# One more transfer cut in two near the end of a decode attention kernel

## The chip, the cores and the metric

The kernel runs on one core of one Trainium2 chip. The metric is device time in microseconds (us), measured over several executions; lower is better.

Times "at" some us are counted from the start of the profiled span. A ratio is the mean time of one kernel's fast runs over that of the other's of the same rounds, so it is not quite the ratio of the medians quoted.

## The reference

One query per head attends to 8192 keys, for 16 heads of width 256, in bf16:

```python
B, H, Sq, Sk, D = 1, 16, 1, 8192, 256
def reference(q, k, v):
    scores = jnp.einsum("bhqd,bhkd->bhqk", q, k) * D ** -0.5
    p = softmax(scores, axis=-1)
    return jnp.einsum("bhqk,bhkd->bhqd", p, v)
```

K and V are 67 MB each and each element is used once. The kernel is a stream from memory with work hung on it.

## The kernel before

Each head's K and V is split into two halves of 2 MB (128 partitions x 32 columns x 256 elements). The halves are numbered: V28 and V29 belong to head 14, V30 and V31 to head 15. One queue, issued from SP (the sync engine), loads them in a fixed order; the last loads are V28, V29, V30, V31. A half normally comes in one transfer, but some come in several, each with its own semaphore (a counter that an engine waits on), so that work can start on the first part:

```python
FIRST_CUT = (4, 4, 8, 16)
LAST_CUT = (16, 8, 4, 4)       # V31, in columns
BEFORE_CUT = (16, 16)          # V30
...
def cuts(kind, n):
    if kind == "k" and n == 0:
        return FIRST_CUT
    if kind == "v" and n == NIT - 1:      # NIT = 32
        return LAST_CUT
    if kind == "v" and n == NIT - 2:
        return BEFORE_CUT
    return (HALF,)                        # 32 columns, 2 MB
```

The scores are made mostly on the vector engine (DVE), partly on TensorE (PE). The scalar engine (ACT) makes the exponentials and copies the outputs. The product with V is made on PE, one matmul for each column of a half. A matmul waits for the transfer that holds its column:

```python
def pv(n, c0=0, c1=HALF):
    ...
    for c in range(c0, c1):
        ...
        pe(lambda e, ...: e.matmul(a[0:1, 0:D], lhsT=E[:, col:col+1],
               rhs=Vb[slot][:, c*D:(c+1)*D], start=..., stop=...), ...,
           [f"e{h}", first_free] + landed("v", n, c, c + 1))
```

After the last keys the order of work on PE is fixed:

```python
n = 2 * (H - 2)
pv(n)                          # V28
softmax(H - 1)                 # transpose m of head 15
pv(n + 1, 0, HALF // 2)        # V29, first 16 columns
softmax2(H - 1)                # broadcast the maximum of head 15
pv(n + 1, HALF // 2, HALF)     # V29, last 16 columns
lmm(H - 1)                     # sum of head 15
n += 2
final(H - 2)                   # ACT: output of head 14
...
pv(n)                          # V30
pv(n + 1)                      # V31
final(H - 1)                   # ACT: output of head 15
```

## Time and profile before

| | before |
|---|---|
| median of 6 runs | 325.15 us (324.94 to 325.31) |
| busiest compute engine | DVE, 86% of the span |
| DMA engines | full in nearly every slice, 416 GB/s over the span |

From the page of the kernel before, its second part: the span in 40 equal slices, busy tenths for each engine, granted clock, busy share of the 16 DMA engines, and what they moved.

```profile
PE   1554328766586858686987756886665966668897
DVE  3799999999999999999998988889988889888600
PEclk9999999999698998989595989777989697897799
DMA  7999999999999999999999999999999999999993
GB/s 276 421 436 428 421 430 428 424 426 426 431 428 426 428 428 428 432 426 424 432 426 434 426 424 430 428 428 429 426 430 426 430 427 428 428 426 428 426 417 120
```

The DMA row is full from the second slice to the last but one at about 428 GB/s. The stream is the limit; the Trainium skill ("HBM Reference", Specifications (TRN2)) gives about 425 GB/s for a core that streams alone, and this trace agrees. DVE is busy too, but is done two slices before the end. So only the end of the stream and what follows it can be shortened by a change at the tail.

The trace records when each of a transfer's 16 engines signals its semaphore. The last of the 16 is the landing. Between 60 and 305 us, whole halves landed 4.90 us apart. The end of the stream:

| landing, us | V28 | V29 | V30, parts | V31, parts |
|---|---|---|---|---|
| before | 304.77 | 309.70 | 312.18, 314.66 | 317.16, 318.37, 319.01, 319.65 |

The timeline of PE in the kernel before, last 18 us. The columns are start, length, engine, line, operation, output<-inputs, shapes and count; in brackets stands the idle time before it and what ended that.

```profile
305.73 3.00 PE L607 MATMUL acc<-Vb,E 128*1 128x256 bf16 x26
308.56 0.38 PE L547 MATMUL misc<-ident,m 128*1 128x128 f32 x2
309.74 1.91 PE L607 MATMUL acc<-Vb,E 128*1 128x256 bf16 x16 [0.80 <-DMA Vb<-in_v_dram]
311.58 0.38 PE L558 MATMUL misc<-g,ones_row 1*128 1x1 f32 x2
311.89 1.91 PE L607 MATMUL acc<-Vb,E 128*1 128x256 bf16 x16
313.63 0.19 PE L587 MATMUL misc<-ones_col,lsum 128*1 128x1 f32 x2
313.69 7.17 PE L607 MATMUL acc<-Vb,E 128*1 128x256 bf16 x64
```

PE idles 0.80 us until V29 lands, and this view shows no idle time after that: the last 64 matmuls take 7.17 us, 0.112 us each. The chain of work that ended last (start, length, what) says the same: V29's landing, then PE, then the last copy on ACT.

```profile
285.68 24.02 DMA Vb<-in_v_dram
309.70 0.04 issue
309.74 1.91 PE acc L607 x16
311.65 0.31 PE misc L558 x2
311.96 1.84 PE acc L607 x16
313.80 0.03 PE misc L587 x2
313.83 7.04 PE acc L607 x64
320.87 0.02 issue
320.89 0.47 ACT o L621
```

The weight loads (PEld), at the step from V30 to V31:

```profile
313.66 3.38 PEld L607 LDWEIGHTS acc<-Vb,E 128*1 128x1 bf16 x32
317.20 3.36 PEld L607 LDWEIGHTS acc<-Vb,E 128*1 128x1 bf16 x32 [0.16 <-DMA Vb<-in_v_dram]
```

They run about 0.1 us ahead of the matmuls (the last one for V30 starts at 316.96, its matmul at 317.07), and had to wait 0.16 us for V31's first part, which landed at 317.16. At 0.112 us each, the matmuls were due there at about 317.27 and would not have waited. That is a second deadline, and the prediction put it 0.1 us behind the first.

### The profile page before, as it was taken

The page shows a single profiled execution, that of the slowest core. Times are in us where ns is not written, and L with a number is a line of the kernel's source. Part 1 is how long each engine was busy: PE and PEld are TensorE (multiplying, and loading weights), DVE is VectorE, ACT ScalarE, POOL GpSimd, SP SyncE. Part 2 cuts the span into 40 slices and gives each one's busy share as a digit, 9 for nine tenths or more (in the row PEclk, how much of TensorE's full clock was granted, in tenths as well). Part 3 has the DMA queues.
Part 4 walks back from the last instruction along what each step waited for, and adds up shares of the span by engine and source line. Part 5 has one row for each costly group of instructions (what it writes and reads, how often), then busy time and mean ns, then how long its engine had stood idle before and what let it go on. Part 6 is the DMA issues. An engine that isn't in the chain of part 4 may idle for free.

```text
span 322.9 us, 6455 instructions
## 1 busy us (share of the span) xinstructions
PE 222.2 (69%) x2166; PEld 155.6 (48%) x2166; DVE 277.8 (86%) x1607; ACT 94.1 (29%) x185; POOL 0.2 (0%) x4
## 2 busy tenths in 40 slices
PE   1554328766586858686987756886665966668897
PEld 0333225655364635454564534564543644455565
DVE  3799999999999999999998988889988889888600
ACT  3362321432324242323142242212422123232010
POOL 0000000000000000000000000000000000000000
PEclk9999999999698998989595989777989697897799
DMA  7999999999999999999999999999999999999993
GB/s 276 421 436 428 421 430 428 424 426 426 431 428 426 428 428 428 432 426 424 432 426 434 426 424 430 428 428 429 426 430 426 430 427 428 428 426 428 426 417 120
DMA packets 10271, 134.37 MB, mean 416 GB/s; under 512 B 1154, under 2 KB 1171, under 8 KB 1940
## 3 DMA queue, kind: packets, MB, share of 16 engines
q1 hardware_dynamic: 10224, 134.22, 98.1%
q8 instruction: 5, 0.08, 0.1%
q14 instruction: 6, 0.05, 0.0%
q10 hardware_dynamic: 36, 0.02, 0.0%
HBM read 134.23 MB, written 0.01 MB: 416 GB/s over the span
## 4 chain that ended last, share of the span: by engine, by line
DVE 52%; DMA 37%; PE 5%; issue 5%; DVEq 1%; ACT 0%; SPq 0%
DVE prod L360 48%; DMA Kb<-in_k_dram 19%; DMA Vb<-in_v_dram 18%; PE acc L607 5%; DVE S L360 2%; DVE g L332 1%; DVE colf L286 0%; DVE recip L341 0%; DVEq L145 0%; DVE m L379 0%; ACT o L621 0%; DVEq L138 0%; DVEq L139 0%; SPq L319 0%; PE misc L558 0%
## 5 line engine op out<-in xcount | busy, mean ns | idle before, releaser
L360 DVE CUSTOM_DVE_ANT_0 prod<-Kb,qbc 128x256 bf16<-128x256 bf16 x768 | 269.1, 411 | 24.6 <-DMA Kb<-in_k_dram 15.7
L607 PE MATMUL acc<-Vb,E 128*1 128x256 bf16 x1024 | 147.4, 314 | 8.8 <-DMA Vb<-in_v_dram 8.8
L607 PEld LDWEIGHTS acc<-Vb,E 128*1 128x1 bf16 x1024 | 96.3, 96 | 52.4 <-DMA Vb<-in_v_dram 9.9
L502 ACT ACTIVATE KT<-tp 128x1024 bf16<-128x1024 bf16 x64 | 62.0, 1021 | 118.2 <-PE tp L493 118.2
L360 DVE DVE_READ_ACCUMULATOR2_ANT S<- 128x1 f32 x768 | 56.8, 74 | 0.0
L493 PE MATMUL tp<-identb,Kb 128*128 128x128 bf16 x512 | 38.2, 234 | 7.8 <-DMA Kb<-in_k_dram 7.8
L493 PEld LDWEIGHTS tp<-identb,Kb 128*128 128x128 bf16 x512 | 32.3, 105 | 15.7 <-issue 14.2
L519 PE MATMUL spe<-qcur,KT 128*128 128x1 bf16 x512 | 20.6, 165 | 19.7 <-ACT KT L502 19.7
L558 PE MATMUL misc<-g,ones_row 1*128 1x1 f32 x32 | 7.1, 287 | 36.1 <-DVE g L332 36.1
L519 PEld LDWEIGHTS spe<-qcur,KT 128*128 128x128 bf16 x512 | 16.4, 99 | 24.5 <-ACT KT L502 24.3
L621 ACT ACTIVATE o<-acc,recip 1x256 bf16<-1x256 f32 x16 | 7.4, 464 | 69.4 <-PE acc L607 69.4
L558 PEld LDWEIGHTS misc<-g,ones_row 1*128 1x128 f32 x32 | 5.7, 221 | 39.1 <-DVE g L332 38.8
L547 PE MATMUL misc<-ident,m 128*1 128x128 f32 x34 | 7.1, 293 | 18.6 <-DVE m L379 18.6
L547 PEld LDWEIGHTS misc<-ident,m 128*1 128x1 f32 x34 | 1.9, 82 | 22.0 <-DVE m L379 21.4
L565 ACT ACTIVATE negb<-misc 128x1 f32<-128x1 f32 x16 | 2.7, 171 | 27.4 <-PE misc L558 27.4
L332 DVE TENSOR_REDUCE g<-misc 1x1 f32<-1x128 f32 x17 | 4.7, 274 | 5.2 <-PE misc L547 5.2
L341 DVE RECIPROCAL recip<-misc 1x1 f32<-1x1 f32 x17 | 2.6, 151 | 4.6 <-PE misc L587 4.6
L572 ACT ACTIVATE E<-S,negb 128x64 bf16<-128x64 f32 x16 | 5.6, 348 | 0.7 <-ACT negb L565 0.2
L587 PE MATMUL misc<-ones_col,lsum 128*1 128x1 f32 x34 | 3.2, 164 | 3.7 <-ACT E L572 3.7
L439 ACT ACTIVATE qbc<-qb 128x256 bf16<-128x256 bf16 x14 | 5.6, 400 | 0.0
L532 ACT ACTIVATE S<-spe 128x16 f32<-128x16 f32 x16 | 2.9, 183 | 7.2 <-PE spe L519 7.2
L413 PE MATMUL tp<-q,identb 16*128 16x256 bf16 x15 | 4.1, 406 | 0.6 <-ACT qb L422 0.5
(29 smaller groups left out, 22.7 us busy)
## 6 DMA issues: line engine op xcount, KB each, us to landing
Kb<-in_k_dram SPq DMA_DIRECT2D x31, 2048.0 KB, 24.3
Vb<-in_v_dram SPq DMA_DIRECT2D x30, 2048.0 KB, 29.5
Vb<-in_v_dram SPq DMA_DIRECT2D x3, 1024.0 KB, 16.5
Kb<-in_k_dram SPq DMA_DIRECT2D x1, 1024.0 KB, 8.5
Kb<-in_k_dram SPq DMA_DIRECT2D x2, 256.0 KB, 3.0
Kb<-in_k_dram SPq DMA_DIRECT2D x1, 512.0 KB, 6.5
Vb<-in_v_dram SPq DMA_DIRECT2D x1, 512.0 KB, 12.7
Vb<-in_v_dram SPq DMA_DIRECT2D x2, 256.0 KB, 13.0
```

Of the source, the lines that this page charges most:

```text
L332: lambda e: e.tensor_reduce(g[0:1, s : s + 1], misc[s][0:1, MT0 : MT0 + P], AX.X, ALU.max),
L360: lambda e, slot=slot, c=c, col=col, h=h, r=(ttr - 1) % PROD: e.tensor_tensor_reduce(out=prod[:, r * D : (r + 1) * D], in0=Kb[slot][:, c * ...
L413: lambda e, i=i, src=src: e.matmul(bank[:, i * D : (i + 1) * D], lhsT=src[0], rhs=src[1], start=True, stop=True),
L439: lambda e: e.activation(out=qbc[:, s * D : (s + 1) * D], in_=qb[:, (h - 2) * D : (h - 1) * D], func=ACT.Copy),
L493: lambda e, c=c, hf=hf, i=(b * NH + hf) * P, view=view: e.transpose(view[:, i : i + P], Kb[slot][:, c * D + hf * P : c * D + (hf + 1) * P] ...
L502: lambda e, gn=gn, view=view: e.activation(out=KT[gn % KT_SLOTS][:, :], in_=view[:, 0 : GROUP * D], func=ACT.Copy),
L519: lambda e, b=b, hf=hf, oc=oc, gn=gn: e.matmul(spe[sl(h)][:, oc : oc + 1], lhsT=KT[gn % KT_SLOTS][:, (b * NH + hf) * P : (b * NH + hf + 1) ...
L547: lambda e: e.matmul(misc[s][0:1, MT0 : MT0 + P], lhsT=m[:, s : s + 1], rhs=ident[:, :], start=True, stop=True),
L558: lambda e: e.matmul(misc[s][:, BC0 : BC0 + 1], lhsT=ones_row[0:1, :], rhs=g[0:1, s : s + 1], start=True, stop=True),
L572: lambda e: e.activation(out=E[:, s * J : (s + 1) * J], in_=S[:, s * J : (s + 1) * J], func=ACT.Exp, bias=negb[:, h : h + 1], scale=SCALE, ...
L607: lambda e, c=c, col=col: e.matmul(a[0:1, 0:D], lhsT=E[:, col : col + 1], rhs=Vb[slot][:, c * D : (c + 1) * D], start=(x == 0 and c == 0), ...
L621: lambda e: e.activation(out=o[0:1, h * D : (h + 1) * D], in_=acc[s][0:1, 0:D], func=ACT.Copy, scale=recip[0:1, s : s + 1],),
```

## The change

The intent is to let PE start on V29 half a transfer earlier, and so remove its 0.80 us of idle time. V29 comes in two transfers of 1 MB, as V30 already does; a semaphore is added for its first part.

```diff
-        s_last = [sem(f"s_l{i}") for i in range(len(LAST_CUT) + len(BEFORE_CUT) - 2)]
+        s_last = [sem(f"s_l{i}") for i in range(len(LAST_CUT) + 2 * (len(BEFORE_CUT) - 1) - 1)]
...
-            if kind == "v" and n == NIT - 2:
+            if kind == "v" and n in (NIT - 3, NIT - 2):
                 return BEFORE_CUT
...
-                    s = sem_l[slot] if i == len(cs) - 1 else s_last[i + (len(LAST_CUT) - 1) * (n == NIT - 2)]
+                    s = sem_l[slot] if i == len(cs) - 1 else s_last[i + (len(LAST_CUT) - 2 + NIT - 1 - n if n < NIT - 1 else 0)]
```

The instructions of PE, DVE and ACT and their order are the same in both kernels. SP issues one transfer more, and one PE wait is split in two. (The diff is shortened.)

## The prediction

> **What bounds the kernel.** The page's first part has DVE busy 86%, PE 69%, but its slice table shows the 16 DMA engines full in nearly every slice at 425 to 430 GB/s: 134.22 MB of K and V come through one queue, and that stream is the limit. The landing records of the trace give one 2 MB half every 4.90 us, to the end. The change touches only the last 15 us.
>
> **The tail now** (timeline and landing records, us from the span's start). V28 (first half of head 14) lands at 304.77; V29, the half that is cut, at 309.70; V30 in two 1 MB parts at 312.18 and 314.66; V31 in parts of 1, 0.5, 0.25, 0.25 MB at 317.16, 318.37, 319.01, 319.65. PE finishes V28 and the small transpose of m at about 308.94 and then idles 0.80 us for V29 (timeline, releaser DMA Vb). From 309.74 it never stops: 16 matmuls, the broadcast of g, 16, the sum, then 64 matmuls of head 15, ending at 320.87; the last ACT copy is 320.89 to 321.36. At the full clock granted from 304.2 on, a matmul costs 0.112 us (64 in 7.17), so PE gets through V30 at about 313.69 + 3.58 = 317.27. V31's first part lands at 317.16. The weight loads even show a 0.16 us wait for DMA there. So PE has a second deadline only about 0.1 us behind the first.
>
> **What the change does.** It adds one issue on SP (0.33 us, at about 286.0, when over 20 us of transfers are queued: off the path), one semaphore, and one wait on PE. The order of work on PE, ACT, DVE is unchanged. V29's first half should land 2.47 us before its second, at about 307.2, which is before PE asks for it. The 0.80 us wait vanishes: PE starts V29 at 308.95 and its second half (due 309.70) is there by 310.8.
>
> **Where that goes.** All later PE work moves 0.8 us earlier until it meets V31: V30's second part (314.7) is needed at about 314.7, and PE is done with it at about 316.5. Then it must wait about 0.7 us for V31's first part, which cannot come earlier, since the DMA stream sets it. From 317.2 on 32 matmuls x 0.112 = 3.6 us follow, ending at 320.8. Gain at most 0.1 us. Against it: cutting costs the stream a little. V30's pair took 4.96 us, uncut halves 4.90 to 4.93, so V31 should land about 0.04 us later. The Trainium skill, "DMA: Bandwidth & Descriptors", Rules for kernel authors, asks for at least 1 MiB per DMA for bandwidth; the parts are just that, and this trace agrees that the loss is about 1%. Net: -0.05 us, within the noise of 324.94 to 325.31.
>
> **Time:** 325.15 us, 8 in 10 between 324.6 and 325.7. Faster by over 2%: 0.005; within 2%: 0.99; slower: 0.005.
>
> **What would show it.** Right: the idle of PE before V29 at 309 is gone or under 0.1 us; a new wait of PE for DMA Vb of 0.5 to 0.8 us shows at about 316.5, before the last 32 matmuls; the chain of waits ends in DMA Vb landing at about 317.2, PE x32, ACT, with x64 gone; V31's landings are where they were, within 0.15 us. Wrong: V29's first part lands after 308.9; the last 64 matmuls still run without a gap and end 0.5 us or more earlier (then V31 came earlier); or V31 lands 0.3 us or more later.
>
> **What would make it wrong.** A lower granted clock in the last 18 us (half clock was granted in 3.4 us spells until 304.2, and a spell there costs up to 1.7 us), or the extra transfer costing the queue more than the 0.05 us seen on V30.

## The result

| | before | after |
|---|---|---|
| median of 6 runs each | 325.15 us (324.94 to 325.31) | 325.20 us (324.65 to 325.47) |
| ratio of the means | 1 | 1.0001 (95%: 0.9988 to 1.0014) |
| V28's landing | 304.77 | 304.55 |
| V29's landing, its parts | 309.70 | 307.04, 309.53 |
| V30's landing, its parts | 312.18, 314.66 | 312.01, 314.50 |
| V31's first part, V31's last part | 317.16, 319.65 | 317.00, 319.50 |
| V28's landing to V31's first part | 12.39 us | 12.45 us |
| V28's landing to the start of the last ACT copy | 16.12 us | 16.19 us |

The time is the same. The last row is the measure of the tail used below. V28 is the last half that no kernel but one cuts, and counting from it takes out most of the scatter of the stream's earlier part.

The timeline of PE after, in the same stretch:

```profile
305.72 2.78 PE L607 MATMUL acc<-Vb,E 128*1 128x256 bf16 x24
308.34 0.38 PE L547 MATMUL misc<-ident,m 128*1 128x128 f32 x2
308.55 1.91 PE L607 MATMUL acc<-Vb,E 128*1 128x256 bf16 x16
310.39 0.38 PE L558 MATMUL misc<-g,ones_row 1*128 1x1 f32 x2
310.70 1.91 PE L607 MATMUL acc<-Vb,E 128*1 128x256 bf16 x16
312.44 0.19 PE L587 MATMUL misc<-ones_col,lsum 128*1 128x1 f32 x2
312.50 3.95 PE L607 MATMUL acc<-Vb,E 128*1 128x256 bf16 x32
317.05 3.65 PE L607 MATMUL acc<-Vb,E 128*1 128x256 bf16 x32 [0.59 <-DMA Vb<-in_v_dram]
```

The 0.80 us wait before V29 is gone. Counted from V28's landing, V29 starts 4.00 us after it (308.55 - 304.55) and not 4.97 (309.74 - 304.77), so 0.97 us was freed. It is lost again in two places. V30's 32 matmuls take 3.95 us where 32 unhindered ones take 3.65. And a new wait of 0.59 us stands before V31. The weight loads show both waits, at V30's second part and at V31:

```profile
314.54 1.61 PEld L607 LDWEIGHTS acc<-Vb,E 128*1 128x1 bf16 x16 [0.43 <-DMA Vb<-in_v_dram]
317.04 3.36 PEld L607 LDWEIGHTS acc<-Vb,E 128*1 128x1 bf16 x32 [0.89 <-DMA Vb<-in_v_dram]
```

The chain that ended last now runs through the landing of V31's first part, and V29 is no longer in it:

```profile
305.04 11.96 DMA Vb<-in_v_dram
317.00 0.04 issue
317.05 3.67 PE acc L607 x32
320.71 0.02 issue
320.74 0.47 ACT o L621
```

From this landing to the end of the last matmul are 3.71 us (320.71 - 317.00). In the kernel before they are the same 3.71 us (320.87 - 317.16): there too, V31's first part set the end, though the chain named V29.

### The profile page after: what moved, and what is told of

It is laid out like the page before. It is cut to its first block, busy times and chain, and to the rows that moved or that the text cites. A ratio compares the mean times of both kernels' runs of the same rounds, so it can differ in the third digit from the quotient of the medians.

```text
span 322.8 us, 6456 instructions
## 1 busy us (share of the span) xinstructions
PE 220.3 (68%) x2166; PEld 155.1 (48%) x2166; DVE 277.7 (86%) x1607; ACT 94.1 (29%) x185; POOL 0.2 (0%) x4
## 4 chain that ended last, share of the span: by engine, by line
DVE 49%; DMA 42%; issue 5%; PE 3%; DVEq 0%; ACT 0%; SPq 0%
DVE prod L360 46%; DMA Kb<-in_k_dram 27%; DMA Vb<-in_v_dram 15%; PE acc L607 3%; DVE S L360 2%; DVE g L332 0%; DVE colf L286 0%; DVE recip L341 0%; DVE m L379 0%; DVEq L145 0%; ACT o L621 0%; DVEq L138 0%; SPq L319 0%; DVEq L139 0%; DVEq L142 0%
## 5 line engine op out<-in xcount | busy, mean ns | idle before, releaser
L360 DVE CUSTOM_DVE_ANT_0 prod<-Kb,qbc 128x256 bf16<-128x256 bf16 x768 | 269.1, 411 | 24.5 <-DMA Kb<-in_k_dram 15.1
L607 PE MATMUL acc<-Vb,E 128*1 128x256 bf16 x1024 | 144.7, 310 | 8.7 <-DMA Vb<-in_v_dram 8.5
L607 PEld LDWEIGHTS acc<-Vb,E 128*1 128x1 bf16 x1024 | 95.0, 95 | 50.7 <-DMA Vb<-in_v_dram 9.9
L493 PE MATMUL tp<-identb,Kb 128*128 128x128 bf16 x512 | 38.9, 237 | 7.1 <-DMA Kb<-in_k_dram 7.1
L493 PEld LDWEIGHTS tp<-identb,Kb 128*128 128x128 bf16 x512 | 33.0, 106 | 15.2 <-issue 12.8
L422 ACT ACTIVATE qb<-tp 128x512 bf16<-128x512 f32 x7 | 3.9, 595 | 3.8 <-PE tp L413 3.8
```

Source lines behind the costliest of these rows:

```text
L360: lambda e, slot=slot, c=c, col=col, h=h, r=(ttr - 1) % PROD: e.tensor_tensor_reduce(out=prod[:, r * D : (r + 1) * D], in0=Kb[slot][:, c * ...
L422: lambda e: e.activation(out=qbc[:, a * D : b * D] if first else qb[:, (a - 2) * D : (b - 2) * D], in_=bank[:, 0 : (b - a) * D], func=ACT. ...
L493: lambda e, c=c, hf=hf, i=(b * NH + hf) * P, view=view: e.transpose(view[:, i : i + P], Kb[slot][:, c * D + hf * P : c * D + (hf + 1) * P] ...
L607: lambda e, c=c, col=col: e.matmul(a[0:1, 0:D], lhsT=E[:, col : col + 1], rhs=Vb[slot][:, c * D : (c + 1) * D], start=(x == 0 and c == 0), ...
```

## The experiments

**The theory (deadlines).** Each part of V sets a deadline for the end: its landing, plus about 0.11 us for every column from that part to the end and 0.34 us for the two small products (broadcast and sum) where they lie between. The latest of these sums sets the end. V29's and V31's first part's differed by 0.1 us at most. Moving one leaves the other. **Rival 1 (cost).** The gain was real, but the extra transfer cost the stream as much. **Rival 2 (one limit).** Only V31's first part, or only the stream's end, sets the time, and V29 never mattered.

Nine runs were made (seven new kernels, then the changed kernel and one of the seven again), each with five timed rounds against the kernel before on the same chip. All gave correct results.

### V31 finer, with V29 whole and with V29 cut

```diff
-LAST_CUT = (16, 8, 4, 4)
+LAST_CUT = (8, 8, 8, 4, 4)
```

In the kernel before (V29 whole):

> Kernel before (V29 whole) with only V31 cut finer, (8,8,8,4,4) in place of (16,8,4,4). Deadline theory (PE's tail starts at the later of 'V29 is here' and 'V31's first part is here', so both must come early): PE is busy without a gap from V29's landing at 309.7 to 317.27 and then finds V31 already here, so nothing is gained: 0.0 us, at most 0.1 us faster, and the weight loads' wait at V31 is gone. Rival (the stream's extra transfer costs what the cut wins): about 0.05 us slower. Rival (the late first part of V31 alone sets the end): 0.6 us faster.

In the changed kernel (V29 cut):

> The changed kernel with V31 cut finer as well, (8,8,8,4,4). Deadline theory: PE now reaches V31 at about 316.3 (V30's second part lands at 314.5, 16 matmuls of 0.112 us follow) and finds 8 columns there (about 315.8), so it ends at about 320.1 instead of 320.7: 0.5 to 0.65 us faster than either kernel (0.15 to 0.2%), seen in the profile as the time from V28's landing to the end of the last matmul, 16.2 us before and after, 15.6 here. The wait of 0.59 us before the last 32 matmuls shrinks to under 0.15 us. Rival (extra transfers eat the gain): not faster than before, V31's last landing 0.5 us later.

| | ratio to before (95%) | tail from V28's landing |
|---|---|---|
| V31 finer, V29 whole | 0.9996 (0.9979 to 1.0013) | 16.06 us |
| V31 finer, V29 cut | 0.9981 (0.9965 to 0.9997) | 15.72 us |

V31 finer by itself gains 0.06 us of tail, of which 0.04 us is V29 landing sooner after V28 (4.89 us and not 4.93). V29's cut by itself lost 0.07. Together they gain 0.40. The chain of the first run still begins with V29, and PE still runs 64 matmuls without a gap:

```profile
285.59 24.05 DMA Vb<-in_v_dram
309.64 0.04 issue
309.69 1.91 PE acc L607 x16
...
313.77 7.02 PE acc L607 x64
```

In the second run the chain ends in V31's third part, which landed at 318.43:

```profile
306.04 12.39 DMA Vb<-in_v_dram
318.43 0.04 issue
318.47 1.92 PE acc L607 x16
320.39 0.02 issue
320.42 0.46 ACT o L621
```

Rival 2 falls: V31 alone gains next to nothing, since V29's deadline stands right behind it, and with V31 moved, V29 matters. Rival 1 falls as the cause too, since two extra transfers gained where one did not. The expectation was a little too good: the end came 0.4 to 0.5 us earlier, not 0.5 to 0.65. The new deadline, that third part with 16 columns still to do, landed at 318.43; the expectation had only reckoned with the first part of 8.

### Useless work on PE, in both kernels

Between V29 and V30, after the sum of head 15, PE repeats six matmuls of V29 into an unused part of another bank of PSUM, the memory that PE writes to (the diff is shortened):

```diff
         lmm(H - 1)
+        for i in range(6):
+            pe(lambda e, ...: e.matmul(spe[0][0:1, D:2*D], lhsT=E[...], rhs=vb[...], start=True, stop=True))
         n += 2
```

In the kernel before:

> Kernel before with six useless matmuls (0.67 us at 0.112 us each) on PE between V29 and V30; the result is unchanged. Deadline theory: PE has no slack left from V29 on, so the end comes 0.55 to 0.7 us later (0.2%). Rival (the DMA stream's end alone sets the time): no change.

In the changed kernel:

> The changed kernel with the same six matmuls at the same place. Deadline theory: they fall into the 0.7 us that the cut has freed and that is otherwise spent waiting for V31; the end moves by less than 0.1 us, and the wait of 0.59 us before the last 32 matmuls falls to 0 to 0.3 us. Rival (the 0.8 us were never freed, or PE's own work sets the end): 0.6 us slower, as in the run with the kernel before.

| | ratio to before (95%) | tail | same kernel without the filler |
|---|---|---|---|
| before, with filler | 1.0020 (1.0002 to 1.0037) | 16.72 us | 16.12 us |
| after, with filler | 0.9995 (0.9978 to 1.0012) | 16.16 us | 16.19 us |

The same 0.68 us of work cost 0.60 us before and nothing after. From the two chains, first before with the filler:

```profile
314.30 0.68 PE spe L674 x6
314.98 7.00 PE acc L607 x64
```

Then the timeline of PE after with the filler:

```profile
313.27 0.81 PE L674 MATMUL spe<-Vb,E 128*1 128x256 bf16 x6
313.92 3.66 PE L607 MATMUL acc<-Vb,E 128*1 128x256 bf16 x32
317.80 3.65 PE L607 MATMUL acc<-Vb,E 128*1 128x256 bf16 x32 [0.22 <-DMA Vb<-in_v_dram]
```

The filler fell into the two waits: V30's 32 matmuls now run unhindered in 3.66 us, and 0.22 us of the 0.59 us wait is left. So the change did free time on PE, and nothing used it.

### What a cut costs the stream

Every V half from V0 to V28 is cut in two as well, with one more semaphore for each of the four buffers (a comment stands for the line that picks it):

```diff
-            if kind == "v" and n in (NIT - 3, NIT - 2):
+            if kind == "v" and n < NIT - 1:
                 return BEFORE_CUT
...
+                    # first part: s_vh[slot]; last part: sem_l[slot], as before
```

> The changed kernel with the 29 earlier V halves also in two transfers of 1 MB: the cost of a cut, 29 times. If a cut costs the stream 0.04 to 0.06 us (V29 took 4.93 us whole and 4.97 us cut; V30 cut 4.97 and 4.96), the kernel is 1.2 to 1.7 us slower than before (0.35 to 0.55%) and uncut 2 MB K halves still land 4.90 us after the V part ahead of them. If the cut's cost in V29 was chance, no change. Rival (an extra transfer costs a fixed 0.2 us or more, so it ate the gain): 6 us slower.

The ratio to before was 1.0062 (1.0049 to 1.0075), 2.03 us between the means. Against before it has 30 cuts more, so one costs 0.068 us. Its trace agrees: over 24 of each, a V half in two parts took 4.964 us to land after the half ahead of it, a whole K half 4.901. The tail kept its length, 16.20 us. The expectation of 1.2 to 1.7 us was too low, because I had taken 0.04 to 0.06 us per cut from single halves. Rival 1 has a true core, 0.07 us, but it is less than a tenth of the 0.97 us freed. By the traces this cost is all that the change did to the tail. The page's DMA issues of this kernel (size and median time from issue to landing) confirm what was run:

```profile
Vb<-in_v_dram SPq DMA_DIRECT2D x63, 1024.0 KB, 28.0
Kb<-in_k_dram SPq DMA_DIRECT2D x31, 2048.0 KB, 25.2
```

### V29 cut, V30 whole

```diff
-            if kind == "v" and n in (NIT - 3, NIT - 2):
+            if kind == "v" and n == NIT - 3:
                 return BEFORE_CUT
```

> The changed kernel with V30 whole again, so that V29 alone is cut. Deadline theory: PE may start V30 only when all of it is here, about 314.5, and 64 matmuls of 0.112 us then run without a gap, so V31's first part is no longer waited for and the end is at about 321.7, 1.0 us later than after and 0.85 us later than before (0.2 to 0.35% slower). The wait before V30 is 1.8 to 2.1 us. Rival (V31's landing alone sets the end): as after.

The ratio to before was 1.0039 (1.0023 to 1.0055), and the tail was 17.18 us, 0.99 us longer than after (1.0 was expected) and 1.06 us longer than before (0.85 was expected). From its timeline:

```profile
315.01 7.15 PE L607 MATMUL acc<-Vb,E 128*1 128x256 bf16 x64 [1.91 <-DMA Vb<-in_v_dram]
```

V30 landed whole at 314.88 and all 64 matmuls came behind it. The same number of cuts as before, in the wrong half, is slower. The stream itself ended no later: V31's last part landed 14.79 us after V28, and 14.88 in the kernel before. Which part's deadline comes last decides.

### Finer still

```diff
-LAST_CUT = (16, 8, 4, 4)
+LAST_CUT = (10, 8, 6, 4, 2, 2)
 BEFORE_CUT = (16, 16)       # V29
+BEFORE_CUT2 = (16, 8, 8)    # V30
```

(The diff is against the kernel before and shortened; the comments are added here.)

> The changed kernel with V30 in (16,8,8) and V31 in (10,8,6,4,2,2), so that no part that lands leaves PE more work than the stream needs for the parts after it. Deadline theory: in the run with V31 in (8,8,8,4,4) the part of 8 that landed at 318.43 left 16 matmuls, 1.8 us, and V30's second part at 314.64 left 48, 5.4 us; both go. The end of the last matmul should be about 15.1 to 15.4 us after V28's landing (15.7 there, 16.1 to 16.2 before and after), 0.7 to 0.9 us faster than before; PE's own chain from V28 allows no earlier end than about 15.1. If the five extra transfers cost more than 0.1 us each, nothing is gained over (8,8,8,4,4).

(The kernel has four transfers more than the kernel before, two more than the one with V31 in five parts; not five.)

The ratio to before was 0.9993 (0.998 to 1.0005) and the tail 15.59 us. The last matmul ended 15.56 us after V28's landing, where 15.1 to 15.4 was expected. That was a miss. The last part landed 15.12 us after V28, later than with V31 in five parts (15.00). From its chain:

```profile
316.53 1.25 PE acc L610 x10
317.78 0.02 issue
317.80 2.64 PE acc L610 x22
320.44 0.02 issue
320.47 0.47 ACT o L624
```

I had reckoned with PE's own chain and forgotten two things. V31's parts still held PE: the second landed at 317.76 and left 22 columns, 2.64 us, and within these the third, landed at 318.69 with 14 columns left, held the weight loads for another 0.20 us and the matmuls for 0.07 us. And the stream's end itself stands 15.1 us after V28, with two matmuls behind it. With the extra cuts that end came 0.13 us later. Over the five-part V31 the tail gained 0.13 us, which the timed rounds don't resolve.

### Side by side

The five-part V31 with V29 cut was the version that beat both, so it ran again beside the changed kernel on one chip.

> The changed kernel once more, on the same chip as the run that follows, so that the two can be compared directly. Same as before within 0.15%; from V28's landing to the end of the last matmul 16.1 to 16.25 us, as in the first trace (16.17).

> The changed kernel with V31 in (8,8,8,4,4), once more beside the changed kernel. Deadline theory: 15.65 to 15.75 us from V28's landing to the end of the last matmul, and a time 0.3 to 0.7 us (0.1 to 0.2%) under both the kernel before and the changed one. If the 0.19% of the first run was chance: no difference in time, and 16.1 us in the trace.

| | median of 5 | ratio to before (95%) | tail |
|---|---|---|---|
| after | 325.14 us | 1.0009 (0.9995 to 1.0023) | 16.14 us |
| after, V31 in (8,8,8,4,4) | 324.63 us | 0.9993 (0.998 to 1.0007) | 15.74 us |

The means of the two differ by 0.51 us (325.20 and 324.69), and the traces by 0.40 us (0.47 us the first time). Against the kernel before, the interval of this second run includes 1; that of the first did not. The traces repeat within 0.05 us, so I hold the gain of about 0.4 us over both kernels for shown in the trace and supported by the times. In the timed ratios to before it is 0.19% and 0.07%.

## Why the prediction was right

The time alone shows little: a gain of 0.5 us would also have fallen into the stated 324.6 to 325.7 us. What speaks for the prediction is that the wait went, the new wait came and the chain changed as it said.

- **The limit.** It said that the DMA stream bounds the kernel and that the change touches only the tail. The full DMA row is the same after, and the tail is where all differences were found.
- **The wait removed.** It said that V29's first part lands at about 307.2 and that the 0.80 us wait goes. The part landed at 307.04, and PE went straight on.
- **The size of what is freed.** It said 0.8 us; it was 0.97. I had taken the modelled end of the small transpose (308.94) as the earliest start of V29. Matmuls overlap in the trace: after the change V29's first one started at 308.55, while the transpose is shown as running until 308.72.
- **Where it goes.** It named V31's first part as the next deadline, about 0.7 us of new wait there. It was 0.59 us, and another 0.3 us was lost at V30's second part, which the prediction had called due just in time (314.7): PE came to it about 0.4 us sooner than that. The prediction put V31's deadline 0.1 us behind V29's; by the single records it was the later one by about 0.025 us, so there was nothing to gain at all. The two filler runs show that this time is slack; the two V31 runs show that V31's first part is what held it.
- **The cost.** It gave a cut 0.04 us. From V28's landing to V31's first part the changed kernel took 0.06 us more, and thirty cuts measured 0.068 us each. The Trainium skill's advice of at least 1 MiB per transfer ("DMA: Bandwidth & Descriptors", Rules for kernel authors) is consistent with that: a pair of such transfers lost 1.3% of 4.90 us.
- **The net.** It said -0.05 us and 325.15 us; measured were +0.03 us between the means and a median of 325.20 us. The sign is within the noise. The trace's tail, 0.07 us longer, has the size of the cut's cost, with no gain set against it: the up to 0.1 us that the prediction allowed was not there. One of its signs, V31's landings within 0.15 us of where they were, was missed by 0.01 us from the span's start (317.16 and 317.00); counted from V28 it holds (0.06 us).

The clock risk it named did not come: PE was granted its full clock in the last 18 us of both traces. (Of the earlier half-clock spells in the kernel before, some lasted 6.8 us and not 3.4.)

What stays open is why single executions scatter by up to a microsecond and more. In every trace the first of the 16 engines signalled V28 at 301.4 to 302.2 us (the kernel with all V cut apart), but the last one 2.8 to 3.7 us later. Only the full 16 means that all data has landed, as the Trainium skill says ("DMA: Bandwidth & Descriptors", Why a DMA increments its semaphore by 16 and not by 1). This trace agrees: PE started V29 at 309.74, 0.04 us after the last of the 16. So the engine that ends last sets every landing. That this lag makes the scatter is an idea, not tested here.

## What to carry to other kernels

Before removing a wait on the chain that ended last, write down for every later arrival its landing plus all work left behind it; the gain is at most the distance from the latest of these sums to the next, and nothing if the removed wait belongs to an earlier one. Here the wait was 0.8 us, the gain was put at 0.1 us, and it turned out as nothing. Of two level deadlines the chain view named one here and hid the other. If two sums are close, move both in one change, and expect each alone to look useless. To learn whether a wait is slack, put that much useless work there: if the time stays, a shorter path to that wait gains nothing.

## What the Trainium skill lacked or had wrong

- "DMA: Bandwidth & Descriptors" (Measured) gives 341 GB/s, 78%, for a transfer of 1 MB. That was measured on transfers issued from another engine (GpSimd), so the page is not wrong, but the figure doesn't carry over. In a queue kept full from SP, 1 MB parts landed 2.48 us apart, about 422 GB/s, and cutting a 2 MB transfer in two cost only 0.068 us. The page lacks this cost of a cut in a full queue.
- The same page says that the 16 engines finish independently, but not by how much in a long stream. Here the last one signalled a transfer 2.8 to 3.7 us after the first, more than half of a 2 MB transfer's 4.90 us, and the whole halves ahead of it show the same spread. In the kernel before, this lag was 0.6 us for the transfer that landed at 3.3 us, and between 2.9 and 3.2 us for all that landed after 40 us; it did not keep growing.
- No page says how to choose the sizes of the last parts of a stream. By these runs the sums of landing and remaining work decide: (16,8,4,4) for the last half gave a tail of 16.2 us, (8,8,8,4,4) 15.7 us, and a finer one only 0.13 us less: its third part left 14 columns and not 16, and its extra cuts delayed the stream's end by 0.13 us (15.12 us after V28 and not 15.00).
